# Mamba-2 SSD with a GELU layer on one core: other fillers at the start, two more in the second rows, and earlier weight joins

## The chip, the core and the metric

The kernel runs on one core of a Trainium2 chip. A core has five engines with their own instruction streams: TensorE (PE in the profile) multiplies matrices, VectorE (DVE) and ScalarE (ACT) work elementwise, GpSimd (POOL) does small elementwise work and issues transfers, and SyncE (SP) issues most transfers. TensorE writes to PSUM, eight banks of 2 KB per partition; the other data lie in SBUF, 128 partitions wide. The engines run at once and wait for one another through semaphores. The metric is the device time of one execution in microseconds (us); shorter is better.

## The reference

Two stages. The first is a state-space recurrence over x of shape (4 batches, 8 heads, 768 steps, 32), with decays `a` and matrices `B`, `C` of 16 columns; the second is a feed-forward layer over 3072 tokens of 256 features, with 2048 hidden features.

```python
for c in range(768 // 32):                      # chunks of 32 steps
    cum = np.cumsum(log_a[:, :, sl], axis=-1)
    L = np.exp(cum[..., :, None] - cum[..., None, :]) * causal
    M = np.einsum('bhin,bhjn->bhij', Cc, Bc) * L
    y_intra = np.einsum('bhij,bhjd->bhid', M, xc)
    y_inter = np.einsum('bhin,bhnd->bhid', Cc, state) * np.exp(cum)[..., None]
    y[:, :, sl] = y_intra + y_inter
    state = np.exp(la.sum(-1))[..., None, None] * state + (Bx decayed to the end of the chunk)
x = y.transpose(0, 2, 1, 3).reshape(3072, 256)
h = x @ w_in                                    # 256 x 2048, double precision in memory
g = h / (1 + np.exp(-1.702 * h))
out = g @ w_out                                 # 2048 x 256
```

`w_in` and `w_out` arrive as 64-bit floats, so the kernel reads them as pairs of 32-bit words and turns them into 32-bit floats itself.

## The kernel before

The 3072 tokens are worked in six groups of 512: group g takes steps 128 g to 128 g + 127 of all four batches. A group consists of two pairs of batches (p = 2 g and 2 g + 1). The kernel works the recurrence in chunks of 64 steps; a pair's 128 steps are two sides of 64. Each group goes through the recurrence and then through the two linear layers. From early in the second group on, the linear layers use a scheme with seven products instead of eight, and the next group's recurrence is interleaved with them. The order of work on each engine is the order in which the program issues it.

**The start (group 0).** `mask_banks` puts a large negative number where j > i (L516, a matmul of an identity with `below`); `differ_of` adds differences of cumulated logarithms (L522, many small matmuls that use 32 rows of the array each) and `rows_first` adds rows (L511). ScalarE takes the exponent (L552), `score` multiplies C and B blocks (L620), VectorE weighs the decays with the scores (`weigh`, L631). Before L522's input `cum` is there, TensorE runs fillers, whose results nobody reads: `plain` (L441, bf16, 256 columns, the whole array), `pads` (L430, 32-bit, 32 x 32 of the array and four columns), and `dense` (L434, 32-bit, the whole array, 64 columns for each of its n). The fillers write into parts of PSUM banks that the work uses later or beside it. In the profile each 32-bit matmul is two records (two passes).

**The rows of group 0.** `finish(..., (0,))` computes the first pair's products with its own steps (`intra`, L745) with a `dense` of 256 columns ahead of each half t of the features. `gain` computes the states' increments (L651), ScalarE keeps them (`keep_first`, L667). `finish(..., (1,))` then does, for each half t: the second pair's `intra` for k = 0 and k = 1, a copy of side 0 by ScalarE (`copied`, L757), the products with the state (`inter`, L732), and the copy of side 1. The four results y0_0 to y0_3 have a PSUM bank each; `begun_y["banks"]` lists them. The copies make `yT`, the input of the first linear layer.

**The weights.** Ten pieces (`PIECES`): four of two column blocks, two of four column blocks of `w_in`, and four pieces of `w_out`. Transfers (`fetch`, on SyncE's queue) bring them as words. VectorE takes the exponent field (`fields` step 0, L203) and the mantissa field (step 1, L206), adds the low word (`rounded`, L231), ScalarE clamps the exponent (`clamp`, L224 and L226), and VectorE joins sign, mantissa and exponent (`join`, L245 and L251), which writes `w_in` or `w_out`. Pieces 0 and 1 are worked in halves before the first layer, the rest by `narrow(i)` from inside the loop over the hidden blocks: `narrow(2)` after block 1, `narrow(3)` after 2, `narrow(4)` after 4, `narrow(5)` after 6. After its join some pieces' successors are fetched into the freed buffers.

**The first linear layer of group 0.** `hidden(0, f)` computes hidden block f (of 16) in two steps k: out of `w_in[:, f, k]` and 512 tokens, in one, two or four matmuls (L806), by `n`, and ScalarE applies the activation (L810). `project_all` is the second layer (L904), and the recurrence of group 1 is interleaved with it; L732 and L745 occur there again, for group 1.

Of the kernel before, what the change touches and what calls it, by code (L numbers as in the profile page):

```python
# [16 lines left out]
P = 128  # L17
# [18 lines left out]
def kernel(  # L36
# [43 lines left out]
    NK = DM // P  # L80
    NF = DF // P
# [68 lines left out]
    PIECES = [("in", f, 2) for f in range(0, 8, 2)] + [("in", 8, 4), ("in", 12, 4)] \  # L150
# [107 lines left out]

    def narrow(i):
        rounded(i)  # L260
        if i == 2:
            join(i)
            fields(i + 1)
            return
        if i + 1 < len(PIECES):
            fields(i + 1)
        join(i, 2 if i == 4 else 1)


    scratch = dram.tile([NC, 2, NB * NH, H], FP32, name="scratch")  # L270
# [155 lines left out]
    def pads(n, t, start=True):  # L426

        for i in range(n):
            c = 32 * (i % R)
            nc.tensor.matmul(out=t[c:c + 32, :4], lhsT=ones[:32, :32], rhs=ones[:32, :4],  # L430
                             start=start, stop=True, tile_position=(0, c), skip_group_check=True)
# [6 lines left out]
    def plain(t, n, start=True):  # L438

        for i in range(n):  # L440
            nc.tensor.matmul(out=t[:, :2 * P], lhsT=nc.const_aps.tensor(1.0, [P, P], BF16),  # L441
                             rhs=nc.const_aps.tensor(1.0, [P, 2 * P], BF16),
                             start=start, stop=True, skip_group_check=True)
# [254 lines left out]
    def finish(pairs, steps=range(2)):  # L698


        g, first = divmod(pairs[0], PG)
        early = pairs[0] < PG
        if 0 in steps:
            if early:
                banks = begun_y["banks"] = [bank(f"y0_{i}") for i in range(4)]
                y = [t[:, :2 * P].rearrange("p (k i) -> p k i", i=H) for t in banks]
                begun_y[0] = [[y[2 * t + i] for t in range(NK)] for i in range(2)], set()
            else:
                both = area(f"y{pairs[0]}")[:, :, :len(pairs) * 2 * H].rearrange(
                    "p (s t) (k i) -> p s t k i", s=2, i=H)  # L710
                begun_y[pairs[0]] = [[both[:, i, t] for t in range(NK)] for i in range(2)] + [both], set()
        y, begun = begun_y[pairs[0]]

        def begin(i, t, parts):
            new = not begun & {(i, t, q) for q in parts}
            begun.update((i, t, q) for q in parts)
            return new

        def inter(n, p, ts=range(2)):

            b = place(p)[1]
            for k in range(2):
                for i in range(2):
                    if g == 0 and i == 0:
                        continue
                    old = (state[g][:, 0] if i else state[g - 1][:, 1])[:, b + k]
                    for r in range(R):
                        t = r // 2
                        if t not in ts:
                            continue  # L730
                        rows, to = slice(32 * r, 32 * r + 32), Q * D * (r % 2)
                        nc.tensor.matmul(  # L732
                            out=y[i][t][to:to + Q * D, 2 * n + k], lhsT=old[rows],
                            rhs=st[p]["CsT"][rows, k, SIDES[i]],
                            start=begin(i, t, range(Q * (r % 2), Q * (r % 2) + Q)), stop=early,
                            tile_position=(32 * r, to), skip_group_check=True)

        def intra(n, p, ts=range(2)):
            L = Ls[p]
            for k, t in [(k, t) for t in ts for k in range(2)] if early else [  # L740
                    (k, t) for k in range(2) for t in ts]:
                for q in range(HB):
                    h = t * HB + q
                    for i, side in enumerate(SIDES):
                        nc.tensor.matmul(  # L745
                            out=y[i][t][D * q:D * q + D, 2 * n + k], lhsT=rx[p][side, k, h],
                            rhs=L[side, k, h // Q, h % Q],
                            start=begin(i, t, (q,)), stop=not early, tile_position=(H * i, D * q),
                            skip_group_check=True)

        cols = slice(2 * first * P, 2 * (first + len(pairs)) * P)

        if first == 0 and g not in yT:
            yT[g] = ffn.tile([P, NK, TG], FP32, tag="yT", name=f"yT{g}")
        if early:
            def copied(i, t):
                nc.scalar.activation(  # L757
                    yT[g][:, t, cols].rearrange("p (k s i) -> p s k i", s=2, i=H)[:, i], y[i][t],
                    AF.Copy)

            if 0 in steps:
                for t in range(NK):
                    dense(begun_y["banks"][0][:, 2 * P:])
                    intra(0, pairs[0], (t,))
                return
            for t in range(NK):
                intra(1, pairs[1], (t,))
                copied(0, t)
                for n, p in enumerate(pairs):
                    inter(n, p, (t,))  # L770
                copied(1, t)
        else:
            for step in steps:
                for n, p in enumerate(pairs):
                    (inter, intra)[step](n, p)
            if 1 not in steps:
                return
            for i in range(2):
                nc.scalar.activation(  # L779
                    yT[g][:, :, cols].rearrange("p t (k s i) -> p s t k i", s=2, i=H)[:, i], y[2][:, i],  # L780
                    AF.Copy)
        state.pop(g - 1, None)
        for p in pairs:
            st.pop(p)
            Ls.pop(p)
# [11 lines left out]
    def hidden(g, f):  # L797
        j, i = divmod(f, 2)
        if i == 0:
            block(g, j)  # L800
        h = bank(f"h{g}_{f}")
        for k in range(NK):
            n = 1 if g or NK * f + k < 5 else 4 if NK * (NF - f) - k <= 13 else 2
            for e in range(n):
                cols = slice(e * TG // n, (e + 1) * TG // n)
                nc.tensor.matmul(out=h[:, cols], lhsT=w_in[:, f, k], rhs=yT[g][:, k, cols],  # L806
                                 start=(k == 0 and e == 0), stop=(k == NK - 1),
                                 skip_group_check=True)

        nc.scalar.activation(gT[g, j][:, i], h, AF.Silu, scale=GELU_SCALE)  # L810
# [258 lines left out]
        differ(p, [(r, ab[p, r]) for r in range(R)])  # L1069

    busy = bank("busy")
    plain(busy, 6)
    both = area("ab0")
    for r in range(R):
        mask_banks(0, r, both[:, r])
    seconds = [bank(f"ab1_{r}") for r in range(R)]
    for r in range(R):
        mask_banks(1, r, seconds[r])
    plain(both[:, 0, 2 * P:], 6, False)
    pads(26, both[:, 0, 2 * P:], False)  # L1080
    differ_of(0)
    turn_blocks(0, "C")
    fetch(0, held=nc.vector, halves=(0,))
# [188 lines left out]
    k = NF // 2 - 1  # L1272
# [110 lines left out]
```

## Time and profile before

| what | value |
|---|---|
| median of three runs | 350.54 us |
| the three runs | 349.5, 350.54, 350.57 us |
| the profiled execution | 350.41 us, its span 348.7 us |
| TensorE busy | 343.4 us, 98% |
| VectorE busy | 257.0 us, 74% |
| ScalarE busy | 149.7 us, 43% |
| TensorE's waits in all | 2.0 us, 0.8 of them before its first instruction |
| first hidden block (L806) starts | 17.41 us |
| second layer (L904) starts | 48.50 us |

The page shows one profiled execution, with times from the start of the span. A group of instructions is a line of the kernel, an engine, an operation and what it writes and reads; L12 is line 12 of the kernel before. A duration is that of one instruction; matmuls are pipelined, so a stream of them runs at a shorter pitch than their duration. The answer on waits gives who waited, for whom, the total in us, how often, and the longest. The chain in order of time gives the start, the length and the work, followed back from the last instruction. In the timeline, a line is a start, a length, the engine, the line, what it writes and reads, and how often; in brackets is the idle time ahead of it and what ended it.

### The profile page before, as it was taken

The numbers are of one execution on the slowest core, as the hardware profiler recorded it, in microseconds if no ns is written. First come the engines' busy times: TensorE is split into PE (matmuls) and PEld (weight loads), VectorE is DVE, ScalarE is ACT, GpSimd is POOL, SyncE is SP. The second block draws the span as 40 slices with busy tenths as digits, with TensorE's granted clock in tenths as the row PEclk, the third lists the DMA queues.
The fourth block names the chain that finished last, engine by engine and source line by source line (L and its number), as shares of the span: only waits on it lengthen the run. The fifth ranks groups of instructions, "written<-read, shape, count | busy, mean of one in ns | idle before, by whom it ended". The sixth has DMA issues, their size and how long they took to land.

```text
span 348.7 us, 8549 instructions
## 1 busy us (share of the span) xinstructions
PE 343.4 (98%) x3514; PEld 281.9 (81%) x3514; DVE 257.0 (74%) x484; ACT 149.7 (43%) x335; POOL 45.2 (13%) x82
## 2 busy tenths in 40 slices
PE   9999999999999999999999999999999999999996
PEld 6757974545688888888888888888888888899996
DVE  7699999999699997839985648986554654455463
ACT  5579674005354313744342544432544322554320
POOL 8305820300396000000000000000000000000000
PEclk9999999999999999999999999999999999999999
DMA  4798995623629000455122336120000120000221
GB/s 103 205 303 265 298 159 134 90 61 76 104 67 155 2 0 12 80 120 97 27 36 61 47 86 113 23 31 8 0 4 2 19 32 12 0 2 0 33 31 60
DMA packets 82831, 25.79 MB, mean 74 GB/s; under 512 B 68856, under 2 KB 81144, under 8 KB 82792
## 3 DMA queue, kind: packets, MB, share of 16 engines
q1 hardware_dynamic: 79912, 23.19, 31.1%
q0 software_dynamic: 1888, 1.74, 2.5%
q8 instruction: 27, 0.44, 0.5%
q10 hardware_dynamic: 992, 0.33, 0.4%
q14 instruction: 12, 0.10, 0.1%
HBM read 21.99 MB, written 3.24 MB: 72 GB/s over the span
## 4 chain that ended last, share of the span: by engine, by line
PE 93%; ACT 3%; DVE 2%; issue 1%; DVEq 0%
PE acc L964 28%; PE X L862 19%; PE Y L872 14%; PE o L904 8%; PE acc L971 7%; PE h L806 6%; PE y L745 2%; PE cb L620 2%; PE y L732 2%; PE ab L522 1%; ACT p L226 1%; ACT p L224 1%; PE A L651 1%; PE ab L516 0%; DVE m L231 0%
## 5 line engine op out<-in xcount | busy, mean ns | idle before, releaser
L867 ACT ACTIVATE ac<-X 128x256 f32<-128x256 f32 x76 | 29.1, 383 | 79.8 <-PE X L862 79.4
L964 PE MATMUL acc<-mg,mw 128*128 128x256 f32 x192 | 54.5, 379 | 0.0
L991 DVE TENSOR_TENSOR gT<-Y,ac 128x512 f32<-128x512 f32 x38 | 26.2, 690 | 37.3 <-PE Y L872 33.6
L839 ACT ACTIVATE gT<-gT 128x512 f32<-128x512 f32 (+1 forms) x76 | 39.3, 519 | 31.6 <-DVE gT L991 31.0
L862 PE MATMUL X<-my,mi 128*128 128x256 f32 x152 | 45.1, 379 | 0.0
L991 DVE TENSOR_TENSOR gT<-Y,b 128x256 f32<-128x256 f32 x38 | 15.8, 418 | 34.4 <-PE Y L872 34.4
L964 PEld LDWEIGHTS acc<-mg,mw 128*128 128x128 f32 x192 | 36.5, 190 | 5.0
L806 PE MATMUL h<-yT,w_in 128*128 128x128 f32 (+2 forms) x186 | 36.7, 354 | 0.8 <-DVE w_in L251 0.4
L964 PE MATMUL acc<-gT,w_out 128*128 128x256 f32 x128 | 35.5, 379 | 0.0
L806 PEld LDWEIGHTS h<-yT,w_in 128*128 128x128 f32 x186 | 26.9, 191 | 9.5 <-issue 6.4
L862 PEld LDWEIGHTS X<-my,mi 128*128 128x128 f32 x152 | 28.0, 190 | 3.7
L904 PE MATMUL o<-gT,w_out 128*128 128x512 f32 x64 | 28.6, 597 | 0.0
L830 DVE TENSOR_TENSOR mg<-gT 128x512 f32<-128x512 f32 x40 | 27.2, 680 | 0.0
L964 PEld LDWEIGHTS acc<-gT,w_out 128*128 128x128 f32 x128 | 24.2, 190 | 3.4 <-ACT yT L779 0.2
L867 ACT ACTIVATE b<-X 128x256 f32<-128x256 f32 x38 | 14.6, 384 | 20.6 <-PE X L862 20.2
L862 PE MATMUL X<-yT,w_in 128*128 128x256 f32 x76 | 23.2, 389 | 0.0
L872 PE MATMUL Y<-yT,w_in 128*128 128x256 f32 x76 | 22.7, 381 | 0.0
L872 PE MATMUL Y<-my,mi 128*128 128x256 f32 x76 | 22.6, 379 | 0.0
L862 PE MATMUL X<-my,w_in 128*128 128x256 f32 x76 | 22.6, 381 | 0.0
L872 PE MATMUL Y<-yT,mi 128*128 128x256 f32 x76 | 22.5, 379 | 0.0
L904 PEld LDWEIGHTS o<-gT,w_out 128*128 128x128 f32 x64 | 11.8, 190 | 13.2 <-issue 12.7
L1023 POOL DMA_DIRECT2D out_dram<-ob x32 | 17.4, 551 | 26.5 <-DVE ob L1018 26.2
(143 smaller groups left out, 581.8 us busy)
## 6 DMA issues: line engine op xcount, KB each, us to landing
a<-scratch SPq DMA_DIRECT2D x18, 256.0 KB
bits<-in_moe_w_out_dram SPq DMA_DIRECT2D x8, 512.0 KB
x<-in_x_dram SPq DMA_DIRECT2D x20, 128.0 KB
bits<-in_moe_w_in_dram SPq DMA_DIRECT2D x8, 256.0 KB
bits<-in_moe_w_in_dram SPq DMA_DIRECT2D x4, 512.0 KB
out_dram<-ob SPq DMA_DIRECT2D x128, 16.0 KB
af<-in_a_dram SPq DMA_DIRECT2D x20, 64.0 KB
zC<-in_C_dram SPq DMA_DIRECT2D x36, 32.0 KB
```

The costliest lines, as they stand in the source:

```text
L620: nc.tensor.matmul(out=s["cb"][side, r, k].rearrange("p (q i) -> p q i", q=Q), lhsT=BT[rows, k, side], rhs=CT[rows, k, :, side], start=Tru ...
L806: nc.tensor.matmul(out=h[:, cols], lhsT=w_in[:, f, k], rhs=yT[g][:, k, cols], start=(k == 0 and e == 0), stop=(k == NK - 1), skip_group_ch ...
L830: nc.vector.tensor_tensor(out=t[:, 0:2], in0=B[:, :, 1], in1=B[:, 0], op=ALU.subtract)
L839: nc.scalar.activation(o, i, AF.Silu, scale=GELU_SCALE)
L862: nc.tensor.matmul(out=s["X"], lhsT=lhsT, rhs=rhs, start=i == "1", stop=i == "4", skip_group_check=True)
L867: nc.scalar.activation(copy, s["X"], AF.Copy)
L872: nc.tensor.matmul(out=o, lhsT=lhsT, rhs=rhs, start=s.pop("new", False), stop=i != "5", skip_group_check=True)
L904: nc.tensor.matmul(out=o[c], lhsT=w_out[:, c, f], rhs=gT[g, f // 2][:, f % 2], start=(f == 0), stop=(f == NF - 1), skip_group_check=True)
L964: nc.tensor.matmul(out=acc[g][0][i], lhsT=w, rhs=h, start=(j == 0 and (i, 0) in begins), stop=(j == NF // 2 - 1), skip_group_check=True)
L971: nc.tensor.matmul(out=o[k] if type(o) is list else o[:, cols], lhsT=h[:, cols], rhs=w, start=(j == 0 and (i, k) in begins), stop=(j == NF ...
L991: nc.vector.tensor_tensor(out=o, in0=v, in1=w, op=ALU.add)
L1023: (nc.sync if g else nc.gpsimd).dma_start(out=rows[:, b, :, cols], in_=t[32 * r:32 * r + 32, b * P:(b + 1) * P].rearrange("p (u e) -> p u ...
```

## The change

Four edits. In `narrow`, piece 2's join is split in two halves, and from piece 3 on the join stands between the next piece's exponent field and its mantissa field instead of behind both. A function `spare` runs a `dense` of 128 columns into the unused half of y0_0's bank; it is called once in the second pair's `intra`, in half t = 0 between k = 0 and k = 1, and once behind the copy of side 0 of half 0. In `hidden`, the pieces of 128 columns begin with block 6 instead of the second step of block 9. At the start, six `plain` fillers become two `plain` and a `dense` of 192 columns; behind the masks, six `plain` and 26 `pads` become two `dense` of 256 columns and 12 `pads`.

On TensorE the order of the other instructions is the same. In the built program the second `spare` waits for ScalarE's copy of y0_0; L732 behind it waited for ScalarE's L667 before. The orders on ScalarE, POOL and SyncE are the same.

```diff
--- before.py
+++ after.py
@@ -258,13 +258,11 @@
 
     def narrow(i):
         rounded(i)
-        if i == 2:
-            join(i)
-            fields(i + 1)
-            return
+        if i > 2 and i + 1 < len(PIECES):
+            fields(i + 1, (0,))
+        join(i, 2 if i in (2, 4) else 1)
         if i + 1 < len(PIECES):
-            fields(i + 1)
-        join(i, 2 if i == 4 else 1)
+            fields(i + 1, (1,) if i > 2 else range(2))
 
 
     scratch = dram.tile([NC, 2, NB * NH, H], FP32, name="scratch")
@@ -735,10 +733,15 @@
                             start=begin(i, t, range(Q * (r % 2), Q * (r % 2) + Q)), stop=early,
                             tile_position=(32 * r, to), skip_group_check=True)
 
+        def spare():
+            dense(begun_y["banks"][0][:, 2 * P:], 2)
+
         def intra(n, p, ts=range(2)):
             L = Ls[p]
             for k, t in [(k, t) for t in ts for k in range(2)] if early else [
                     (k, t) for k in range(2) for t in ts]:
+                if early and n and not t and k:
+                    spare()
                 for q in range(HB):
                     h = t * HB + q
                     for i, side in enumerate(SIDES):
@@ -766,6 +769,8 @@
             for t in range(NK):
                 intra(1, pairs[1], (t,))
                 copied(0, t)
+                if t == 0:
+                    spare()
                 for n, p in enumerate(pairs):
                     inter(n, p, (t,))
                 copied(1, t)
@@ -800,7 +805,7 @@
             block(g, j)
         h = bank(f"h{g}_{f}")
         for k in range(NK):
-            n = 1 if g or NK * f + k < 5 else 4 if NK * (NF - f) - k <= 13 else 2
+            n = 1 if g or NK * f + k < 5 else 4 if NK * (NF - f) - k <= 20 else 2
             for e in range(n):
                 cols = slice(e * TG // n, (e + 1) * TG // n)
                 nc.tensor.matmul(out=h[:, cols], lhsT=w_in[:, f, k], rhs=yT[g][:, k, cols],
@@ -1069,15 +1074,17 @@
         differ(p, [(r, ab[p, r]) for r in range(R)])
 
     busy = bank("busy")
-    plain(busy, 6)
+    plain(busy, 2)
+    dense(busy, 3)
     both = area("ab0")
     for r in range(R):
         mask_banks(0, r, both[:, r])
     seconds = [bank(f"ab1_{r}") for r in range(R)]
     for r in range(R):
         mask_banks(1, r, seconds[r])
-    plain(both[:, 0, 2 * P:], 6, False)
-    pads(26, both[:, 0, 2 * P:], False)
+    for k in range(2):
+        dense(both[:, k, 2 * P:], 4, False)
+    pads(12, both[:, 0, 2 * P:], False)
     differ_of(0)
     turn_blocks(0, "C")
     fetch(0, held=nc.vector, halves=(0,))
```

## The prediction

> **What bounds the kernel now.** I read the page first, then TensorE's waits, then the chain in order of time, then rows of the first 17 us.
>
> ```profile
> span 348.7 us, 8549 instructions
> PE 343.4 (98%) x3514; PEld 281.9 (81%) x3514; DVE 257.0 (74%) x484; ACT 149.7 (43%) x335; POOL 45.2 (13%) x82
> ```
>
> TensorE is busy 98% of the span, so only three things can move the end: its few waits, instructions added to or taken from its stream, and the speed at which it runs. Its waits in the whole execution:
>
> ```profile
> PE busy L441 <- PEq L1367: 0.8, 1, 0.8
> PE h L806 <- DVE w_in L251: 0.4, 1, 0.4
> PE h L806 <- ACT p L226: 0.3, 1, 0.3
> PE y L732 <- ACT S L667: 0.3, 1, 0.3
> PE y L745 <- DVE L L631: 0.2, 1, 0.2
> ```
>
> 0.7 us are waits of the first linear layer for weights (the one put down to ACT ends with a w_in join of 32.07 to 33.26, so it is a weight too). Nothing after 33.4 us makes TensorE wait. The chain, from its answer in order of time:
>
> ```profile
> 5.26 0.84 PE ab L430 x52
> 6.11 4.17 PE ab L522 x96
> 10.28 0.22 PE ab L511 x8
> 10.50 1.15 PE cb L620 x63
> ...
> 18.20 0.52 ACT p L224
> 18.72 0.02 issue
> 18.74 0.51 ACT p L226
> 19.25 0.02 issue
> 19.27 1.28 ACT L316
> ```
>
> TensorE leads until the scores (L620); then VectorE, and from 18.20 ScalarE, which clamps exponents for VectorE's joins, carry the chain to 33.4. VectorE is over 90% busy from there to 75 us. The speed shows in L522, the same shape before and after 9.4 us (duration min/median/max in ns):
>
> ```profile
> L522 PE MATMUL ab<-minus,cum x16: 416/416/577, 7.1 to 7.9; 32*128 32x128 f32 x16
> L522 PE MATMUL ab<-minus,cum x16: 267/278/560, 9.4 to 10.0; 32*128 32x128 f32 x16
> ```
>
> So TensorE ran at about half speed until close to 9.8 us. (The granted clock reads 1.00 in those windows; before its first record that column says nothing, the durations do.) Two more places matter below, ScalarE's spare time before its clamp and VectorE's last operand for L732:
>
> ```profile
> 18.20 0.51 ACT L224 ACTIVATE p<-p,edge 128x256 f32<-128x256 uint32 x1 [0.29 <-DVE p L203]
> ```
> ```profile
> 70.46 2.34 DVE L631 TENSOR_TENSOR L<-L,cb 128x1024 f32<-128x1024 f32 x2
> ```
> ```profile
> 73.47 1.16 PE L732 MATMUL y<-CsT,S 32*64 32x64 f32 x64
> ```
>
> The profiled execution took 350.41 us (span 348.7 and 1.7 around it), the median of the runs shown is 350.54, and one run was 349.5. The sum is made against 350.41.
>
> **Opening fillers.** Removed ahead of L516: four bf16 fillers at 0.213 (eight L516 of that shape take 1.71 us), 0.85 us. Added: one 32-bit filler of 192 columns. Its shape at full speed is L434, where a pass of 256 columns runs 0.219; two passes of 192 columns at half speed are 0.66. L516 does not come sooner for it, since `below` on POOL ends at 2.06 and L516 already starts at 2.10: 0. Removed ahead of L522: six bf16 fillers, 1.28 us, and 14 of 26 four-column fillers, 14/26 of 0.84 = 0.45. Added: two 32-bit fillers of 256 columns, four passes of 0.43 = 1.72. Net 0, to +0.15 for the switch of weights. L522 can't start before the scan of `cum` anyway (5.13 + 0.69 = 5.82; it starts at 6.04).
>
> What is bought is not the length but perhaps the speed. The trace shows half speed through 4.2 us of dense bf16 work and 0.8 us of tiny fillers, and full speed after 3.4 us of L522. In the changed kernel dense work lasts to about 5.6 us and the thin stretch shrinks from 0.84 to 0.39. If the clock opens near 6.4, L522 and L511 need some 2.8 us for their 4.4: four groups at the full-speed pitch of 0.11 with 0.2 us per switch. Then ScalarE bounds the scores: L597 ends at 7.75, the exponent L552 takes 1.02, so L620 starts at 8.9 at the earliest, for 10.43: -1.5 at most. Each us of later opening returns about 0.37 (1.6 of gain over 4.4 us). Lower end 0, or +0.15 if nothing opens sooner. I take -1.2, an opening within a us of L522's start, nearer the upper end because the run of 349.5 beside 350.5 looks like such an opening. Transfers allow it: the first half of piece 0 is used by VectorE at 13.6 with no wait on a DMA, and VectorE waited for no DMA before 60 us.
>
> The Trainium skill ("TensorE: Matmul & The Clock Gate", Part 1, "What's actually happening") says that the array clock is doubled after one busy window of some 3.4 us, that the windows run freely, and that the turning point varies from run to run. By that rule alone the kind of filler is no matter and this term is 0. The trace does not follow it to the letter: the array was fed without a break from 0.84 to 5.1, 4.2 us, and half speed lasted to 9.8.
>
> **Fillers in the second rows.** Two 32-bit fillers of 128 columns: one in pair 1's first half between k = 0 and k = 1, one behind the copy of y0_0. Each is two passes of 0.11 and two switches of the whole array's weights (0.1 to 0.15; around L434 TensorE loses 0.15 before and 0.09 behind), 0.41. The first delays L745's k = 1 (15.17) by 0.41. The second adds a wait: it writes the bank that ScalarE's first copy L757 reads, and in the built program it waits for that copy. Queued behind it on TensorE are L732, pair 1's second half and h_0. The copy moves from 15.60 to 16.01 and ends at 16.40; with 0.14 to wake and the filler's 0.31, L732 starts at about 16.8 for 15.81: +0.96, less if the switches hide (low end +0.4). Without the wait it would be +0.4. Cover on TensorE is the weight waits, 0.4 + 0.3.
>
> Who waits for that: ScalarE's other three L757 end at 18.87 for 17.91. They stand ahead of the clamp of 18.20, which had 0.29 to spare, so the clamp, the table load and the next clamp slip by 0.67, and VectorE's join of 21.74, which waited for that clamp, slips with them.
>
> **Joins.** Piece 2's join is split: two L245 and two L251 of 256 elements (0.42 each) for one each of 512 (0.69), 0.27 us more of VectorE once overlaps are allowed for, and its first half is ready some 0.5 sooner. From piece 3 on the join stands ahead of the mantissa (L206, 0.6): same work, weights 0.6 sooner. Both together remove TensorE's two weight waits: -0.75. No DMA is moved past another; the fetches behind joins go out at most 0.6 sooner.
>
> **Pieces of 128 columns** in h_6, h_7, h_8 and half of h_9: sixteen passes of 0.112 for eight of 0.216, 0.07 per h, 3.5 times: +0.2. Nothing hides it once the waits are gone.
>
> **Sum.** TensorE's own path behind the opening: +0.96 - 0.75 + 0.2 = +0.4. VectorE's path: 0.67 + 0.27 = 0.94 later, and it is busy without a gap until L631, which ends at 72.80 and feeds L732 of 73.47; 0.67 of slack there less some 0.1 to wake leaves 0.94 - 0.55 = +0.4. The two don't add; I take +0.45. 350.41 - 1.2 + 0.45 = 349.7.
>
> **Rivals.**
> 1. *The clock opens where it did*, because 32-bit dense work counts no more than bf16 or the instant hangs on something else: 350.41 + 0.1 + 0.45 = 351.0. For it: 4.2 us of dense fillers did not open it. Against: a longer dense stretch and less of the thin one. The rule of the Trainium skill's page "TensorE: Matmul & The Clock Gate" quoted above stands on this side.
> 2. *The opening comes at once and the second rows cost little*: -1.5, fillers +0.4, waits gone -0.75, pieces +0.2: 348.8. For it: TensorE's idle 0.3 ahead of L732 can hide a switch. Against: the added wait on the copy is in the program.
> 3. *The other side: the second filler's wait reaches the end whole.* VectorE 0.94 later at L251 means that h_8's weights come no sooner than TensorE; if the L251 of 32.07, stretched to 1.19 beside POOL's clip of 31.82, is stretched again, TensorE waits there after all. Price: 0.96 + 0.2 and no wait regained, without the opening: 350.41 + 0.1 + 1.16 = 351.7. It turns slower than the bound when under 0.1 of the 0.75 is regained and the clock gives nothing.
>
> **How the numbers follow.** About 0.3%, 1.05 us, is what a measurement of this kernel can tell from no change: 349.49 and 351.59 are the edges. Forecast 0.55 (349.2 to 350.3), rival 1 0.23 (350.6 to 351.4), rival 2 0.12 (348.5 to 349.2), rival 3 0.10 (351.4 to 352.0). Faster: all of rival 2 and a quarter of the forecast, 0.26. Slower: rival 3 and a little of rival 1, 0.13. Same: 0.61. The range leaves out the far ends of rivals 2 and 3: 348.7 to 351.4.
>
> **What the profile after would show.** L522's duration falls from 416 to 270 ns near 6.4 us rather than 9.8, and L620 starts near 9.2. Ahead of L732 TensorE waits for ACT yT L757 instead of ACT S L667. No wait on L251 at h_4, none or one at h_8. L732 of the next pair starts at 73.47 plus the shift of the end, with a wait on DVE L631 before it. Wrong if L522 changes at another time than said, if the filler waits less than 0.3 us for the copy, or if TensorE waits for bits, which would mean transfers don't follow the earlier start.

## The result, and the profile after

The changed kernel is slower: 351.27 us (median of 22 executions, 349.34 to 353.59) against 349.98 for the kernel before (22 executions, 349.5 to 351.04) on the same chip; the ratio is 1.0033, with a 95% interval of 1.0017 to 1.0048. Its executions fall into two kinds: ten with a mean granted clock of 0.999 or 1.000 took 349.34 to 350.59 (median 349.9, as before), twelve with 0.989 to 0.995 took 351.03 to 353.59. "Closed" below means an execution with a mean clock under 0.997, in which the gate that sets TensorE's clock went back to half speed for a while. The profiled execution took 351.69, its span is 350.0, its clock 0.995.

The start of the scores (line numbers of the early functions are two lower after the change: L520, L618, L629, L730 are L522, L620, L631, L732 of before; L748 and L760 are L745 and L757) and all of TensorE's waits after 3 us, from the profile after:

```profile
8.71 0.95 PE L618 MATMUL cb<-CT,Bt 32*64 32x128 f32 x46
```
```profile
PE y L730 <- issue: 1.0, 1, 1.0
PE y L432 <- ACT yT L760: 0.5, 1, 0.5
PE ab L520 <- DVE cum L369: 0.2, 1, 0.2
PE y L748 <- DVE L L629: 0.2, 1, 0.2
```

The scores start 1.7 us sooner than in the profile of before. The waits for weights are gone, the wait for ScalarE's copy has come, and one is new in kind: 1.0 us of "issue", idle time for which the profile shows no other engine. The timeline of TensorE's second rows (start, length, what; in brackets the idle time ahead):

```profile
14.81 0.49 PE L432 MATMUL y<-ones 128*128 128x128 f32 x2 [0.53 <-ACT yT L760]
15.23 0.27 PE L730 MATMUL y<-CsT,S 32*64 32x64 f32 x1
16.53 0.68 PE L730 MATMUL y<-CsT,S 32*64 32x64 f32 x15 [1.04 <-issue]
...
18.14 5.40 PE L811 MATMUL h<-yT,w_in 128*128 128x512 f32 x8
```

The idle time falls inside one group of 16 small matmuls, between its first and its second. By the first linear layer the lead of 1.7 us has become a lag of 0.7 (18.14 for 17.41). And then the clock; the windows answer for after, its columns being the stretch, its length, busy time (and instructions) of PE, PEld, DVE, ACT and POOL, the granted clock, the share of busy DMA engines and GB/s:

```profile
12.00:14.00 2.00, 2.00 (x92) 1.34 (x95) 1.95 (x6) 1.46 (x4) 1.05 (x4) 1.00 0.94 295
14.00:16.00 2.00, 0.97 (x20) 0.61 (x20) 1.93 (x7) 0.56 (x2) 0.00 (x0) 1.00 0.93 300
16.00:18.00 2.00, 1.47 (x63) 1.31 (x62) 1.90 (x8) 0.68 (x2) 0.00 (x0) 1.00 0.97 307
18.00:20.00 2.00, 2.00 (x11) 1.04 (x7) 0.64 (x3) 1.79 (x5) 0.00 (x0) 0.65 0.90 277
20.00:22.00 2.00, 2.00 (x3) 0.67 (x2) 1.42 (x5) 1.96 (x5) 0.00 (x0) 0.50 1.07 318
```

In the clock's own records it opened at 4.94 us, closed at 18.60 and opened again at 22.01; in between, the first layer ran at half speed. In the profile of before the clock column of these stretches reads 1.00 throughout, as here:

```profile
18.00:20.00 2.00, 2.00 (x6) 0.88 (x5) 1.93 (x7) 1.75 (x3) 0.00 (x0) 1.00 0.73 213
```

**What the idle time is.** The page lists a DMA queue of kind "instruction" with 27 transfers: TensorE's code. In the trace each is 16,384 bytes, and the starved instruction is always among the first three from record 449, from 705 or from a later one a multiple of 256 further on, so a transfer is a block of 256 instructions. In the first 100 us of the kernel before, each transfer starts 0.5 to 2.5 us after TensorE has entered the block ahead of it. There the block that begins with record 705 was fetched at 12.43 us; in the changed kernel at 14.26, though TensorE had passed record 449 at the same time (11.1 and 10.9). What stood ahead of it? SyncE's queue, after and before:

```profile
10.77 7.08 SPq L180 DMA_DIRECT2D bits<-in_moe_w_in_dram  x10
```
```profile
12.49 6.99 SPq L180 DMA_DIRECT2D bits<-in_moe_w_in_dram  x10
```

The weights' loads wait for a one-element write by VectorE (L170, in `fetch`), which stands between its products with the scores. Scores 1.7 us sooner release ten loads of 256 and 512 KB 1.7 us sooner. In the windows answer for before, the two microseconds in which its code was fetched are the emptiest around (0.30, against 0.94 after):

```profile
12.00:14.00 2.00, 1.83 (x39) 0.92 (x36) 2.00 (x8) 0.23 (x2) 1.61 (x6) 1.00 0.30 93
```

The Trainium skill ("Runtime: NRT & Kernel Launch", "Instruction fetch mechanics") says that engines' code comes in blocks of 16 KB, 256 instructions, by the sequencer's own DMA queue while the block before runs, and that the cost is mostly hidden. The trace agrees on the blocks; hidden it is in the profile of before and not here.

### The profile page after: what moved, and what is told of

Same layout as the page of the kernel before. It is cut to its first block, busy times and chain, and to the rows that moved or that the text cites. A ratio compares the mean times of both kernels' runs of the same rounds, so it can differ in the third digit from the quotient of the medians.

```text
span 350.0 us, 8551 instructions
## 1 busy us (share of the span) xinstructions
PE 344.0 (98%) x3514; PEld 282.8 (81%) x3514; DVE 257.8 (74%) x486; ACT 149.4 (43%) x335; POOL 44.6 (13%) x82
## 4 chain that ended last, share of the span: by engine, by line
PE 97%; ACT 1%; DVE 1%; ACTq 1%; issue 0%; DVEq 0%
PE acc L969 28%; PE X L867 19%; PE Y L877 14%; PE h L811 11%; PE o L909 8%; PE acc L976 7%; PE y L748 3%; PE cb L618 2%; PE y L730 2%; PE A L649 1%; PE ab L520 1%; ACTq L130 1%; PE y L432 0%; DVE L L629 0%; ACT L314 0%
## 5 line engine op out<-in xcount | busy, mean ns | idle before, releaser
L811 PE MATMUL h<-yT,w_in 128*128 128x128 f32 (+2 forms) x214 | 38.0, 338 | 0.0
L811 PEld LDWEIGHTS h<-yT,w_in 128*128 128x128 f32 x214 | 28.7, 194 | 8.2 <-issue 6.9
```

## The experiments

Kernels were run in sets, each with the kernel before on the same chip, whose median was 350.08 to 350.28 us. The table holds every kernel; "scores", "first layer" and "second pair" are the starts of L618/L620, of the first hidden block and of L730/L732 at the second pair of batches, in the profiled execution.

| run | median, us | ratio to before, 95% | closed | scores | first layer | second pair | span |
|---|---|---|---|---|---|---|---|
| before, profile shown | | | | 10.43 | 17.41 | 73.47 | 348.7 |
| changed kernel | 351.27 | 1.0017 to 1.0048 | 12 of 22 | 8.71 | 18.14 | 74.70 | 350.0 |
| e1_start_only | 351.68 | 1.0042 to 1.0069 | 4 of 6 | 8.82 | 17.93 | 73.58 | 349.7 |
| e2_spares_only | 350.93 | 1.0018 to 1.0042 | 4 of 12 | 8.97 | 17.95 | 73.66 | 349.0 |
| e3_no_spares | 351.56 | 1.0021 to 1.0066 | 5 of 7 | 8.78 | 18.01 | 75.31 | 350.6 |
| e4_old_start | 354.8 | 1.0123 to 1.016 | 2 of 5 | 8.89 | 17.99 | 73.65 | 354.3 |
| f1_loads_later | 350.67 | 1.0004 to 1.0036 | 3 of 12 | 8.70 | 17.05 | 73.41 | 348.9 |
| f2_more_pads | 351.03 | 1.0014 to 1.0035 | 0 of 7 | 8.93 | 18.11 | 74.06 | 349.3 |
| f3_joins_only | 350.2 | 0.9992 to 1.0009 | 0 of 11 | 8.79 | 16.88 | 72.92 | 348.3 |
| f4_pieces_only | 354.4 | 1.0095 to 1.0125 | 1 of 4 | 10.61 | 17.58 | 73.80 | 354.4 |
| h4_before_loads_early | 352.82 | 1.0056 to 1.0086 | 6 of 6 | 8.73 | 18.58 | 76.10 | 351.4 |
| h2_later_one_spare | 349.65 | 0.9973 to 0.9996 | 0 of 12 | 8.71 | 16.16 | 72.91 | 348.2 |
| h3_later_old_joins | 349.84 | 0.9985 to 1.0033 | 1 of 12 | 9.09 | 17.42 | 73.25 | 348.5 |
| h1_later_one_spare_old_joins | 350.81 | 0.9998 to 1.0048 | 5 of 12 | 8.82 | 16.65 | 73.36 | 348.6 |
| i1_clip_gpsimd | 350.63 | 0.9989 to 1.0027 | 4 of 11 | 8.77 | 16.40 | 73.25 | 348.5 |
| i2_before_clip_gpsimd | 349.96 | 0.9983 to 1.0003 | 0 of 11 | 8.79 | 16.91 | 72.94 | 348.2 |
| i3_joins_one_spare | 350.01 | 0.9986 to 1.0003 | 0 of 11 | 8.72 | 17.42 | 73.06 | 348.3 |
| j1_loads_middle | 349.66 | 0.9974 to 1.0014 | 2 of 11 | 8.98 | 16.30 | 73.00 | 348.4 |
| j2_loads_middle_clip | 349.71 | 0.9974 to 1.001 | 2 of 12 | 8.71 | 18.32 | 74.78 | 350.0 |
| k1_no_late_clip | 349.21 | 0.9957 to 0.9983 | 1 of 12 | 8.80 | 16.08 | 72.77 | 348.2 |

Two readings of the table alone. From the second pair's rows to the end it takes 275.2 to 275.5 us in every kernel but three (e1, e4, f4), so 73 us decides. And the old start (before, e2, e4, f3, f4, h4, i2, i3) has its scores at 8.7 to 9.0 in six of eight profiles: the 10.43 of the profile shown, with the clock opening at 9.80, is the rarer kind.

**The parts of the change.** e1 is before with the diff's two start edits; e2 is before with `spare` and its two calls; e3 is the changed kernel without `spare`; e4 is the changed kernel with before's start.

> The kernel before with the start fillers of the change alone. Theory W (the slow executions come from TensorE's waits in the second rows, which the two fillers there and a late code load make long enough to close the clock gate again): the clock opens near 5 to 6 us, L620 starts near 8.8, no execution shows a mean clock under 0.998, median 0.8 to 1.2 us below before, about 349.0. Rival O (opening early is itself what lets the gate close later, whatever stands in the second rows): a third to a half of the executions at a mean clock of 0.995 or less and at 351 us or more. Rival S (no gain from an early opening, since weights come no sooner): clock 0.999 throughout and within 0.3 us of before.

> The kernel before with the two fillers in the second rows alone. Theory W: opening near 9.8 as before, the second filler waits 0.5 us for the copy, and some executions close the gate (mean clock 0.995 or less, 351 us or more); those at 0.999 are 0.3 to 0.5 us above before. Rival O: no execution under 0.998; 0.3 to 0.5 us above before throughout.

> The changed kernel without the two fillers in the second rows. Theory W: no execution under a mean clock of 0.998, the code load no longer shows as a wait or is under 0.3 us, median 1.0 to 1.5 us below before, about 348.7. Rival O: the same share of executions at 0.995 or less as the changed kernel, median above 350.5.

> The changed kernel with the start fillers of before. Theory W: opening near 9.8, the wait for the copy and closings as in the changed kernel in a part of the executions (mean clock 0.995 or less); the others 0 to 0.5 us above before. Rival O: no execution under 0.998, time within 0.5 us of before.

W falls with e1 and e3, which closed in 4 of 6 and 5 of 7 without the fillers. S, within 0.3 us of before, falls with e1, 1.6 us above it. The start alone is no faster than the whole change, so it is not the fillers in the rows that cost most. O fits e1 and e3, but not the rest: the old start opens the clock early too, at 3.6 to 5.8 us in six of its eight profiles, and the kernel before closed in 2 of the 139 executions beside these runs; e1's profiled execution opened at 5.34 and never closed. e1's two executions that did not close took 351.43 and 351.76, so closing is not all that is slow there: its program is 64 instructions shorter, its later blocks of code end elsewhere, and its profile has further stalls for code, of 0.4 us at 11 us and 0.7 us at 152 us. What e1 and e3 share with the changed kernel is the idle time of issue at record 705 in L730/L732, here in e1 and in e3:

```profile
16.45 0.56 PE L732 MATMUL y<-CsT,S 32*64 32x64 f32 x11 [1.52 <-issue]
```
```profile
15.78 0.64 PE L730 MATMUL y<-CsT,S 32*64 32x64 f32 x11 [1.28 <-issue]
```

e2 and e4, with the old start, have none there, but 0.6 and 0.8 us at record 449 within the scores; and e4 has stalls of 1.3 and 2.0 us at 205 and 260 us, in rows that the change does not touch. That gave theory C, the code.

**Is it the place of a block's end, or what the DMA engines carry?** f1 leaves TensorE alone and moves the write that releases the loads; f2 restores the place of the block's end with fillers; f4 shifts later blocks by adding instructions only.

```diff
 f1 (on after)                                   f2 (on after)
-    fetch(1, held=nc.vector)                   -    pads(12, both[:, 0, 2 * P:], False)
     weigh(0, (slice(1, 2),))                   +    pads(26, both[:, 0, 2 * P:], False)
     ...                                        -  ... else 4 if NK * (NF - f) - k <= 20 else 2
     clamp(0, half=0)                           +  ... else 4 if NK * (NF - f) - k <= 13 else 2
+    fetch(1, held=nc.vector)                    f3: on before, the new `narrow` alone
     for i in range(2, 6):                       f4: on before, `<= 13` becomes `<= 20`
```

> The changed kernel with one thing moved: the first word that VectorE writes into the buffer of the second piece of w_in (the write that lets SyncE issue the weights' loads) comes two products and one clamp later, so the loads start near 12.3 us and not at 10.77 us; TensorE's instructions are untouched. Theory C (TensorE's code arrives in blocks of 256 instructions over the same DMA engines as the weights; the block behind its record 705 was fetched at 14.26 us because the weights' loads stood ahead of it): the fetch comes at 12 to 13 us, the 1.0 us of issue idle at L730 near 15.5 us is gone or under 0.3, the gate closes in none or few of the executions, and the median falls from 351.3 to 349.5 (349.0 to 350.0). Theory B (the place of the block's end in the program is what costs, whatever the DMA engines carry): the idle time stays above 0.8 us and the median at 351.3. Theory W (TensorE's wait of 0.53 us for ScalarE's copy closes the gate): closings in about half of the executions as before, median 351.

> The changed kernel with before's 26 small fillers at the start in place of 12 (56 instructions more) and before's pieces of h (56 fewer), so TensorE's program has the same length and its blocks of code end where they end in the kernel before from the second group on; ahead of the second rows they end 56 instructions sooner in the work than in the changed kernel. Theory C: record 449 falls into the scores, before the weights' loads are released, the next block is fetched near 12 us, no idle time of issue over 0.3 us at L730, few closings, median 349.9 (349.3 to 350.5; 0.3 of it is the 14 fillers' own time). Theory B: the same, since the place is restored. Theory W: the copy is still waited for, closings in half of the executions, median 351.3.

> The kernel before with the joins ahead of the next piece's mantissas alone; TensorE's program is unchanged, so its blocks of code end where they did. The prediction's term for this part: TensorE's two waits for w_in (0.4 us at h_4, 0.3 at h_8) go, 349.3 against 350.0 (349.2 to 349.8). Theory Z (the waits were cover for something that ends last anyway): the waits go and the time stays within 0.2 us of before.

> The kernel before with seven more contraction steps of h in 128-column pieces alone: 56 TensorE instructions more behind the first 40 us. The prediction's term: +0.2 us, 350.2. Theory C: the blocks of code end 56 instructions sooner in the work of all later groups, as they did with 64 in the changed kernel with before's start, where 256 instructions of second rows ran through in 1.6 us and the next block needed over 3; so issue idle of 1 to 2 us near 205 and near 260 us, and 352.5 to 354.5.

In f1 the loads start at 12.47 us, the DMA engines are as empty from 12 to 14 us as in the kernel before, the block comes at 13.10 in place of 14.26, and the row group runs through behind its wait for the copy:

```profile
12.00:14.00 2.00, 2.00 (x100) 1.46 (x99) 1.84 (x7) 1.51 (x4) 1.17 (x4) 1.00 0.31 90
```
```profile
14.71 0.49 PE L432 MATMUL y<-ones 128*128 128x128 f32 x2 [0.53 <-ACT yT L760]
15.13 1.00 PE L730 MATMUL y<-CsT,S 32*64 32x64 f32 x16
```

Closings fall from 12 of 22 to 3 of 12. With TensorE's program unchanged, theory B (the place alone) is out for this stall. The time fell a third as far as C said, from 351.27 to 350.67 and not to 349.5, and the intervals overlap; why comes below. f2 has the stall at 0.4 us and no closing, but took 351.03, over the 350.5 that C and B allowed: its profile has waits of its own (0.6 us for weights, 0.5 for the copy, 0.4 for VectorE) beside the 14 more fillers; which of them cost the rest is not shown. f4 came out as C said, 354.4 for 352.5 to 354.5. TensorE's timeline in f4:

```profile
207.23 0.34 PE L745 MATMUL y<-L,x 64*32 64x64 f32 x13 [1.53 <-issue]
...
262.35 0.34 PE L745 MATMUL y<-L,x 64*32 64x64 f32 x15 [1.70 <-issue]
```

Here it is the place: TensorE passed record 4801 at 203.94 and was at 5057, a block later, by 205.70, while the fetch of that block began at 204.79, took 0.93, and TensorE went on at 207.23. In the kernel before, the same two records lie 4.5 us apart (204.04 and 208.55). A block that consists of small matmuls alone is used up in 1.8 us and needs 3.3 to come.

f3, the joins alone, is 1.000 (0.9992 to 1.0009): theory Z. One of the two waits for weights stayed (0.6 us in its profile); where the rest of the gain went is not shown. Its profile shows something else, though:

```profile
PE cb L618 <- issue: 0.8, 1, 0.8
```

This is a stall for code at record 449, in the scores. All six profiles in which the old start opened early have it, 0.5 to 0.9 us long (e2, e4, f3, h4, i2, i3), and the two that opened late have none: part of what an early opening wins goes there.

**The converse, and the rest of the time.** h4 is the kernel before with nothing changed but the place of the write, now ahead of the scores; h1 to h3 take parts out of f1.

```diff
 h4 (on before)
+    fetch(1, held=nc.vector)
     score(range(PG))
     ...
-    fetch(1, held=nc.vector)
 h2: f1 without the second spare(), pads(13) at the start;  h3: f1 with before's narrow;  h1: both
```

> The kernel before with one thing moved: VectorE's one-element write that lets SyncE issue the loads of w_in's second piece stands ahead of the scores and not between its products, so the loads start near 9.3 us in place of 12.49; no instruction of TensorE changes and no filler. Theory C (the weights' loads ahead of the fetch of TensorE's next block of code starve TensorE): the fetch of the block behind record 705 comes at 13.5 to 14.5 us and not near 12.4, TensorE is idle for 0.7 to 1.5 us on issue at that record (near 16 us), the gate closes in a quarter to a half of the executions, and the median is 350.9 (350.3 to 351.6) against 350.1. Theory D (early weights can only help, and what starves TensorE is the new start): no idle time on issue beyond before's, no closings, 350.1 or a little less.

> The changed kernel with the weights' loads later (as in the run of that name) and without the second filler of the second rows, one small filler more at the start so that the program keeps its length. Theory W+C (both TensorE's stall for code and its 0.53 us for ScalarE's copy make windows in which the gate closes): no closings now (0 or 1 execution with a mean clock under 0.996), spread under 1.5 us. Theory V (VectorE's products for the second pair, ready at 72.8 to 73.3 us whatever TensorE does, release its rows): TensorE stands idle for 1.3 to 1.9 us before them, and the undisturbed time does not fall: 350.3 (349.7 to 350.6). If TensorE's 0.53 us counted to the end: 349.8 or less.

> The changed kernel with the weights' loads later and before's order of joins and mantissas. Theory V: VectorE has one join less ahead of the second pair's products, so they end 0.5 us or more sooner (72.3 to 72.8 where the run with the loads later had 73.27), TensorE's waits for w_in come back (0.3 to 0.8 us in all) but lie inside its idle time ahead of those rows, and the time falls by about 0.5 us: 350.0 (349.6 to 350.4). Theory T (TensorE's waits count): 351.2.

> The changed kernel with the weights' loads later, without the second filler, with before's order of joins: of the change there remain the dense start, the first filler and the 128-column pieces. Theories W+C and V together: no closings, VectorE's products of the second pair end at 72.3 to 72.8 us, TensorE waits there for 0.3 to 1.0 us, 349.6 us (349.2 to 350.0), at or just under before. Theory T: 350.6.

h4 is the clearest of all: no instruction of TensorE changed, no filler, and the kernel before loses 2.7 us, more than the 0.2 to 1.5 that C expected. The block was fetched at 13.80, TensorE stood for 1.9 us, and all six executions closed (profiled: 17.54 to 24.37, two windows). Its SyncE queue and TensorE's timeline:

```profile
9.38 8.86 SPq L180 DMA_DIRECT2D bits<-in_moe_w_in_dram  x9
```
```profile
16.16 0.44 PE L745 MATMUL y<-L,x 64*32 64x64 f32 x27 [1.89 <-issue]
```

h2 came out at 349.65 with no closing, as W+C said, but below the 350.3 of theory V: something of what TensorE's wait for the copy held up did count. The way is the one that the prediction describes: in f1 ScalarE's clamp comes late and VectorE's join waits for it (the first line), so that VectorE's products of the second pair end at 73.26; h2, without the second filler, has no such wait, and they end at 72.76. Still h2's profile shows TensorE waiting 1.30 us for VectorE at the second pair (the second line), as f1's does:

```profile
DVE p L245 <- ACT p L226: 0.6, 1, 0.6
```
```profile
72.91 1.18 PE L730 MATMUL y<-CsT,S 32*64 32x64 f32 x64 [1.30 <-DVE L L629]
```

h3 fits V in its median, though executions of 351.73 and 353.19 at a clock of 1.000, which did not close, stay unexplained; h1 does not fit: 350.81 with 5 closings of 12, though it lacks the copy's wait. Its profile, of an execution that did not close, has 0.6 us for code and 0.9 for weights instead. So the gate closes without the copy's wait too.

**VectorE, and the start without anything else.** i1 (on h2) and i2 (on before) let GpSimd do `clip_rows(1)`, three VectorE operations near 60 us; i3 is before with the new joins and the first `spare`, with `pads(25)`. j1 is the changed kernel without the second `spare`, with `pads(13)` and `fetch(1, ...)` behind the second `weigh(0, ...)`; j2 is j1 with i1's edit. k1 is h2 without GpSimd's two clips of `az` near 30 us, which leaves out that part of the computation.

```diff
 i1, i2                                          k1
-        nc.vector.tensor_scalar(out=t, ...     -        nc.gpsimd.tensor_scalar(out=t, in0=t, scalar1=1e-6, ...
+        engine = nc.gpsimd if g == 1 else nc.vector
+        engine.tensor_scalar(out=t, ...                  nc.gpsimd.memset(...)
 ...  (the copy and the memset behind it go to `engine` too)
```

> The kernel with the loads later and without the second filler, and the clipping of the second group's rows of a (three VectorE operations, 0.87 us from 60.80 to 61.67 there) moved to GpSimd, which stands idle from 47 to 63 us. Theory V (VectorE's products release the second pair's rows): the products end 0.6 to 0.9 us sooner (71.9 to 72.2), TensorE's wait ahead of those rows shrinks from 1.30 to 0.4 to 0.7, and the time falls by as much: 348.9 us (348.6 to 349.2) against the 349.65 without the move. Theory N (what is won there is given back later, or GpSimd's work slows VectorE's): 349.65 or more.

> The kernel before with the same move to GpSimd and nothing else. In its profiled execution TensorE came to the second pair's rows at 73.5 us, 0.7 after VectorE's products. Theory V: VectorE sooner, TensorE unchanged, no gain: 350.1 us (349.9 to 350.2). If VectorE's load costs TensorE elsewhere: 349.6 or less.

> The kernel before with its own start, its own pieces and its own loads, with the new order of the joins and the first filler of the second rows alone (one small filler fewer at the start, for the length of the program). Against the run with the loads later and without the second filler it lacks the dense start. Theory O' (the clock opens between 3.9 and 5.3 us in most executions of the old start too, so that the dense start brings little): 350.0 us (349.7 to 350.3), no closings. Theory P (the prediction's opening term, 1.2 us, once nothing takes it back): 350.6 or more, since the run with the dense start had 349.65.

> The changed kernel without the second filler (one small filler more at the start) and with the write that releases the weights' loads one product later than in the changed kernel, near 11.3 us: between its 10.66 and the 12.2 us of the run with the loads later. The loads later left VectorE waiting 0.3 to 1.5 us for the weights near 16.4 us in three profiled runs. Theory C' (the loads have to start after TensorE's block of code is asked for, near 12.2 us, or so close to it that their first bytes come later): the fetch near 12 to 12.6 us, issue idle at record 705 under 0.6 us, VectorE's wait for the weights near 16.4 us under 0.4, few closings, 349.5 us (349.0 to 350.0). If 11.3 is still too soon: the fetch at 13.5 or later, issue idle of 0.8 to 1.3, closings in a third or more, 350.8 or more.

> The same with the clipping of the second group's rows of a on GpSimd. Theory V, if the fetch is not late: VectorE's products of the second pair end near 72.0 and not 72.8 us, TensorE waits ahead of them for 0.5 us and not 1.3, and it is 0.4 to 0.8 us faster than the same without the move: 348.9 (348.5 to 349.4). Theory N: as fast as that one.

> The kernel with the loads later and without the second filler, with GpSimd's clip of the decays a of the later chunks (two operations, 0.84 and 3.30 us from 29.47 there) left out, a part of the computation. Theory G (VectorE starts 1.7 us sooner than in the kernel before, is level with it at 34.4 us, because an L245 and an L206 take 1.31 and 1.30 us beside that clip and not 0.68 and 0.69): VectorE keeps 0.8 to 1.2 us of its lead, the products of the second pair end at 71.6 to 72.0 and not 72.76, TensorE's wait ahead of the rows falls from 1.30 to under 0.5, 348.8 us (348.5 to 349.3) against 349.65. Theory D' (the weights' transfers, which end when they end, hold VectorE): it waits elsewhere, products at 72.6 or later, 349.6.

i2 shows the one half of V: VectorE's products end at 71.97 in place of 72.80, TensorE comes by itself at 72.94, nothing gained beyond the interval (349.96; 0.9983 to 1.0003). i1 did not show the other half. Up to 50 us it is the program of h2, yet four of eleven executions closed, for none of h2's twelve; in its profile VectorE waited 1.5 us near 16.4 for weights that the later loads brought late. Between "too soon for the code" (10.66) and "too late for VectorE" (12.2) lies a race: j1, at 11.3, had its block at 11.77 and no stall to speak of in its profiled execution, j2, the same up to 50 us, at 14.15 and 2.2 us of stall, the longest of all. Two executions of each closed, one of j1's at a clock of 0.949 with 359.39 us. Six of j2's twelve executions took 348.66 to 349.28; j2's ten that did not close have a median of 349.26 and j1's nine of 349.61: in V's direction, but the intervals of the ratios overlap.

i3 needs no dense start to come out at 350.01, the same as before. Against it, h2, which has the dense start, the pieces of 128 columns and the loads later, took 349.65 beside a kernel before of the same speed (350.10 and 350.16). That is 0.1%, with intervals that overlap, and it is not the start's alone: no more than this is left to see of the prediction's 1.2 us.

k1 has the lowest median, 349.21 (0.9957 to 0.9983, which overlaps h2's interval). In its profiled execution VectorE lost 1.35 us to late weights, and its products of the second pair ended at 72.62, not at the 71.6 to 72.0 of theory G. h2's and then k1's VectorE timelines:

```profile
31.16 1.31 DVE L245 SCALAR_TENSOR_TENSOR p<-bits,p 128x512 uint32<-128x512 uint32 x1
...
33.11 1.30 DVE L206 TENSOR_SCALAR m<-bits 128x1024 uint32<-128x1024 uint32 x1
34.45 1.23 DVE L231 SCALAR_TENSOR_TENSOR m<-bits,m 128x1024 f32<-128x1024 uint32 x1
```
```profile
17.71 0.29 DVE L203 TENSOR_SCALAR p<-bits 128x256 uint32<-128x256 uint32 x1 [1.35 <-DMA bits<-in_moe_w_in_dram]
...
32.16 0.69 DVE L245 SCALAR_TENSOR_TENSOR p<-bits,p 128x512 uint32<-128x512 uint32 x1
...
33.49 0.76 DVE L206 TENSOR_SCALAR m<-bits 128x1024 uint32<-128x1024 uint32 x1
34.28 1.23 DVE L231 SCALAR_TENSOR_TENSOR m<-bits,m 128x1024 f32<-128x1024 uint32 x1
```

Beside GpSimd's clip two instructions of VectorE take 0.62 and 0.54 us more (1.31 and 1.30 for 0.69 and 0.76): this much of theory G is shown. VectorE then stands at 34.45 in h2, with products begun at 10.02, and at 34.51 in the kernel before, with products begun at 11.75: the lead is gone by then. That the late weights and the clip both take from it is shown; which share each has in an undisturbed execution of the changed kernel is not.

## Why the prediction was wrong, step by step

- **Opening fillers, the step that failed.** Its local part was right: the clock opened at 4.94 (predicted near 6.4), L520 took about 270 ns (medians 268 and 270), the scores started at 8.71 (9.2). Over twelve profiles the dense start opened between 4.4 and 6.7 us, so it does what the prediction said it might. The term of -1.2 was not. First, the 4.4 us of slow L522 that it saved are no fixed cost of the kernel before, whose start opened at 3.6 to 5.8 us in six of eight profiles; the prediction took one execution's draw for a property, although it had seen a run of 349.5 and called it "such an opening". The 350.41 that its sum starts from is 0.4 us above the median of 22, 349.98, for the same reason or by chance. Second, the sentence "Transfers allow it" looked only at words that VectorE waits for. It missed whose transfers the released loads collide with: TensorE's own code, 1.0 us of stall in the profiled execution, and the half-speed window behind it, 3.4 us long. Third, the slack of 0.67 between VectorE's products (72.80) and L732 (73.47) was charged against delays and not against gains: where nothing disturbs the start, TensorE waits 1.3 us there (f1, h2). The ten executions of the changed kernel that did not close have a median of 349.9, as before, where the sum has 0.75 less; what the early opening is worth by itself no run isolates.
- **Fillers in the second rows.** The wait for ScalarE's copy is there, 0.53 us. From the scores to L732 it took 5.38 us before and 6.52 after, up to the group's first matmul: +1.1 for the +0.96 forecast. e2, the fillers alone, costs 0.2 to 0.4%, close to that (0.6 to 1.5 us), though four of its twelve executions closed; taking the second one out of f1 gave 0.9 us beside the kernel before (350.67 to 349.65, with 350.23 and 350.10). The slip of ScalarE's clamp, forecast at 0.67, is VectorE's wait of 0.6 us in f1. Rival 3's mechanism was real, but not what decided: e3 has no such filler and is as slow as the changed kernel.
- **Joins.** Both waits for weights are gone in the profiles of the changed kernel, of f1 and of h2, as predicted, but 0.5 to 1.1 us of them stayed in f2, f3, i1, i3, j1 and k1, which have the same joins; alone (f3) the -0.75 was 0.0 (-0.3 to +0.3 us).
- **Pieces of 128 columns.** Up to the second pair's rows f4 is 0.3 us later than before, with the clock opening at 10.15 and 9.80; +0.2 is not contradicted. The +4.2 us of f4 come from later blocks of code: its profile loses 3.2 us to the two stalls, and 3.4 us at half speed follow the second. In the changed kernel these 56 instructions and the 8 of the fillers replace the 64 fewer at the start (7078 records in both kernels), so that the blocks end where they did from the second group on; that none of its parts can be judged alone by its time follows from it.
- **Rivals.** Rival 1 (no gain from the opening, 351.0) has the time nearly right by luck, for its rule was not the reason: the clock opened sooner. The range, 348.7 to 351.4, holds the median by luck too: no case in it has the stall for code, and the likeliest case and the sign were wrong.
- **What would show it wrong** was named in part: "if TensorE waits for bits". TensorE waited for bits of its own program.

## What to carry to other kernels

Fillers and other instructions are not only time: on an engine with thousands of them, their number moves the ends of its blocks of code, and a block of small matmuls can be used up before the next has come; an edit of a few dozen instructions can cost 1% in places that it does not touch (f4). When a change lets an engine work sooner, look at which transfers it releases, and at what was travelling in the empty stretch that they now fill; moving one release (h4) cost more than the whole change. And a gain is bounded by the slack of the engine that ends next to it, while a single profiled execution of a start that varies from run to run is no measure of it.

## What was not expected of the hardware

- **Code.** A fetch takes 0.9 to 2.1 us in the transfers' records, and TensorE goes on 1.3 to 1.6 us after it has ended (after, f4, e1, e3). With weights ahead of it, it starts not 0.5 to 2.5 but 3.4 (after) and 3.6 us (h4) after the block ahead was entered. In e1 and e3 it is 2.2 and 2.5, against 1.3 for the same block in the profile of before; there TensorE used up the block ahead in 3.2 and 3.5 us, so a smaller delay was enough for a stall.
- **The gate.** Apart from the one with which the work ends, every closing in a profiled execution lasted 3.41 or 6.83 us and began a whole number of 3.41 us after the opening (4 times that in after, h4 and j2, 3 times in e3, 74 and 76 times in f4 and e4). The window just ended held the stall whole, but for j2's, of whose 2.2 us 0.2 lay ahead of it. e1's stall of 1.52 us lay across two windows, 0.7 and 0.9, and closed nothing. That fits the rule of the Trainium skill ("TensorE: Matmul & The Clock Gate", Part 1, "What's actually happening") of windows of 3.4 us that run freely, and the spread would follow from it: by the phase of the windows the same stall would close the gate in one execution and not in the next. One profiled execution of each kernel can't show that. Idle time alone is not the measure, since 1.04 us closed the gate in the changed kernel, while f4's 1.53 us at 205.7, e4's 1.32 at 205.5 and the 1.30 that f1 and h2 wait for VectorE near 72 us lay in one window each and closed nothing. The gate closed in 27 of 41 executions of the kernels whose profile shows a stall of over 1 us in the second rows with the loads early (after, e1, e3, h4), 2 of 12 of j2, whose profile has the longest one, 0 of 33 of f3, i2 and i3, and 2 of 139 of the kernel before beside the experiments. What closed it in four of e2's twelve, five of h1's and four of i1's eleven, with no such stall in their profiles, stays open.
